# An attention step with cached keys and values on one core: two value tiles loaded as 120 and 8 rows, and the scores of the last three tiles ahead of their value products

## The chip, the cores and the metric

The kernel runs on one core of a Trainium2 chip. The metric is the time of one execution on the device in microseconds (us), as the median of several runs; less is better. Times in a profile count from the first instruction. The engines are named as in the profile: PE multiplies matrices, DVE and ACT work on vectors, POOL is nearly unused, and SP issues almost all transfers (DMA). Sixteen DMA engines carry the transfers.

## The reference

One decode step: four sequences, one query each, 32 heads, 4096 cached positions, head size 128, all in float32.

```python
x = A_x                                            # (4, 1, 512)
mod = (_silu(c) @ w_mod).reshape(c.shape[0], 6, 1, -1)
sa, ca, ga, sb, cb, gb = (mod[:, i] for i in range(6))
h = _layernorm(x) * (1 + ca) + sa
q = (h @ wq).reshape(4, 1, 32, 128)                # per head
scores = einsum("bhqd,bhkd->bhqk", q, k_cache) * 128 ** -0.5
o = einsum("bhqk,bhkd->bhqd", softmax(scores), v_cache)
x = x + ga * (o.reshape(4, 1, 4096) @ wo)
h = _layernorm(x) * (1 + cb) + sb
x = x + gb * (_silu(h @ w1) @ w2)                  # w1 (512, 1792), w2 (1792, 512)
```

The caches are 256 MB each. All that is read comes to 567 MB, and each byte is read once.

## The kernel before

**Tiles.** The work is cut into N = 64 steps. Step n = 4t + b takes two heads (2t and 2t + 1) of sequence b. Its keys are one tile of 128 partitions with 32 KB each (4 MB): 64 partitions for each head, and in a partition 64 positions of 128 values. Its values are a second tile of the same shape. I call them k*n* and v*n*.

**A step.** DVE multiplies the k tile by the query in two instructions (`mult`, L217). ACT sums 30 of the 64 positions (`red_act`, L223), DVE the other 34 (`red_dve`, L226), and that gives the scores. DVE takes the maximum of each partition (`rowmax`, L230), PE transposes the maxima (`bmax`, L234), DVE takes the maximum for each head and negates it (`negmax`, L241), ACT forms the exponentials (`softexp`, L252), and PE multiplies them with the v tile in 16 matmuls, each run as two passes (`pv`, L265, 32 in the profile). After four steps `finish_a` and `finish_b` divide by the sum and put the result of two heads into `oz`.

**The tail.** `project` multiplies `oz` with wo (L299), tile t by tile t; the first 12 of the 16 are done before the last `pv`. Then come the residual, the second layernorm, w1 (L357), SiLU, w2 (L367) and the output. The layernorm's result, transposed for the matmul with w1, is `h2T`.

**Buffers and order.** All big transfers go through one pool of five buffers of 32 KB per partition (`kv`), issued by SP in the order of the program (`fetch`, L71). A transfer into a buffer waits until the last reader of what was in it is done: a k buffer is freed by DVE and ACT, a v buffer by PE. The order on every engine is that of the program text; no scheduler moves instructions. Up to step 59 the tiles k(n+1) and v(n+1) are requested at the start of step n. For the last steps the order is k61, k62, k63 (at step 60), v61, v62 (at step 61), wo0 (step 62), the first half of wo1 (step 63, start), and, after the exponentials of step 63, v63 in three pieces, the rest of wo1 in two, w1, and w2 in four pieces. wo0 and wo1 are the halves of wo, 4 MB each; w1 and w2 have 3.5 MB each.

Of the kernel before, what the change touches and what calls it, by code (L numbers as in the profile page):

```python
# [17 lines left out]
def kernel(  # L18
# [14 lines left out]
    P = 128  # L33
    B, H, S, Dh = kc.shape
# [7 lines left out]
    NJ = HP * S // P  # L42
# [7 lines left out]
    EPS = 1e-5  # L50
    N = B * NT
    NP = 3

    const = ctx.enter_context(tc.tile_pool(name="const", bufs=1))
    kv = ctx.enter_context(tc.tile_pool(name="kv", bufs=5))
# [4 lines left out]
    def psum(shape, tag, bufs):  # L60
        return ps.tile(shape, F32, tag=tag, name=tag, bufs=bufs)
# [7 lines left out]
    def fetch(t, src, *cuts):  # L69
        for lo, hi in zip(cuts, cuts[1:]):  # L70
            nc.sync.dma_start(t[:, lo:hi], src[:, lo:hi])  # L71

    def load(name, shape, src, *cuts):
        t = kv.tile(shape, F32, tag="kv", name=name)
        fetch(t, src, *(cuts or (0, shape[1])))
        return t

    kt, vt = {}, {}

    def load_k(n):  # L80
        t, b = divmod(n, B)
        src = kc[b, HP * t : HP * (t + 1)].rearrange("h (p j) d -> (h p) j d", p=HALF)
        kt[n] = load(f"k{n}", [P, NJ, Dh], src)

    def load_v(n, *cuts):
        t, b = divmod(n, B)
        src = vc[b, HP * t : HP * (t + 1)].rearrange("h (p j) d -> (h p) j d", p=HALF)
        vt[n] = load(f"v{n}", [P, NJ, Dh], src, *cuts)

    xg = const.tile([P, P], F32, name="xg")  # L90
    cg = const.tile([P, P], F32, name="cg")
# [5 lines left out]
    for g in range(G):  # L97
        nc.gpsimd.dma_start(xg[W * g : W * g + B, :], xr[:, g * P : (g + 1) * P])
    wmt = [load(f"wm{i}", [P, 2, 6 * D], wmv[:, 2 * i : 2 * i + 2, :]) for i in range(2)]
    wqt = [load(f"wq{i}", [P, 2, H * Dh], wqv[:, 2 * i : 2 * i + 2, :]) for i in range(2)]  # L100
    load_k(0)
# [14 lines left out]
    for g in range(G):  # L116
        nc.vector.tensor_scalar(avg[:, g, :], sel, 1.0 / G, None, op0=ALU.mult)
    pz = [const.tile([P, NG * W + W // 2], F32, name=f"pz{i}") for i in range(NP)]
    for t in pz:
# [76 lines left out]
    def make_qb(t):  # L196
        p = psum([P, B, Dh], "q", 2)
        for b in range(B):
            for i in range(HP):
                ch, u = divmod(HP * t + i, CW // Dh)  # L200
                j, g = divmod(ch, G)
                nc.tensor.matmul(  # L202
                    p[HALF * i : HALF * (i + 1), b, :],
                    ident[:, W * g + b : W * g + b + 1].to_broadcast([P, HALF]),
                    qs[:, j, u * Dh : (u + 1) * Dh],
                    start=True, stop=True,
                )
        qb[t] = work.tile([P, B, Dh], F32, tag="qb", name=f"qb{t}")
        nc.scalar.activation(qb[t], p, AF.Copy)  # L209
# [3 lines left out]
    def mult(n, lo, hi):  # L213
        t, b = divmod(n, B)
        if lo == 0:
            sc[n] = work.tile([P, NJ], F32, tag="sc", name=f"sc{n}", bufs=3)
        nc.vector.tensor_mul(  # L217
            kt[n][:, lo:hi, :], kt[n][:, lo:hi, :], qb[t][:, b : b + 1, :].to_broadcast([P, hi - lo, Dh])
        )

    def red_act(n, lo, hi):
        for j in range(lo, hi):
            nc.scalar.activation(kt[n][:, j, :], kt[n][:, j, :], AF.Copy, accum_out=sc[n][:, j : j + 1])  # L223

    def red_dve(n, lo, hi):
        nc.vector.tensor_reduce(sc[n][:, lo:hi], kt[n][:, lo:hi, :], axis=AX.X, op=ALU.add)  # L226

    def rowmax(n):
        nm[n] = work.tile([P, 1], F32, tag="rm", name=f"rm{n}", bufs=3)
        nc.vector.tensor_reduce(nm[n], sc[n], axis=AX.X, op=ALU.max)  # L230

    def bmax(n):
        p = psum([P, P], "mx", 2)
        nc.tensor.transpose(p, nm[n].to_broadcast([P, P]), ident)  # L234
        nm[n] = p

    def negmax(n):
        t = work.tile([P, 1], F32, tag="nm", name=f"nm{n}", bufs=3)
        for i in range(HP):
            h = slice(HALF * i, HALF * (i + 1))  # L240
            nc.vector.tensor_reduce(t[h], nm[n][h, h], axis=AX.X, op=ALU.max, negate=True)  # L241
        nm[n] = t

    def softexp(n):
        t, b = divmod(n, B)
        if b == 0:
            rs[t] = work.tile([P, B], F32, tag="rs", name=f"rs{t}", bufs=3)
        o = W // 2 - JJ
        for i in range(HP):
            h = slice(HALF * i, HALF * (i + 1))  # L250
            w = pz[n % NP][h, : NG * W].rearrange("p (g w) -> p g w", w=W)
            nc.scalar.activation(  # L252
                w[:, :, o + i * W // 2 : o + i * W // 2 + JJ],
                sc[n][h].rearrange("p (g j) -> p g j", j=JJ),
                AF.Exp, bias=nm[n][h], accum_out=rs[t][h, b : b + 1],
            )

    def pv(n):
        t, b = divmod(n, B)
        if b == 0:  # L260
            po[t] = psum([P, JJ * Dh], "po", 2)
        o = W // 2 - JJ - JJ * b
        for j in range(NG):
            g = j % G
            nc.tensor.matmul(  # L265
                po[t][W * g : W * (g + 1), :],
                pz[n % NP][:, j * W + o : (j + 1) * W + o],
                vt[n][:, JJ * j : JJ * (j + 1), :].rearrange("p j d -> p (j d)"),
                start=(b == 0 and j < G), stop=(b == B - 1 and j >= NG - G),
            )  # L270

    def finish_a(t):
        o = work.tile([P, JJ, Dh], F32, tag="o", name="o")
        nc.vector.tensor_copy(o, po[t].rearrange("p (j d) -> p j d", j=JJ))  # L274
        d = psum([P, 1 + HP, B], "small", 1)
        nc.tensor.matmul(d[:, 0, :], blk, rs[t], start=True, stop=True)
        for i in range(HP):
            for r in range(HP):
                for j in range(JJ):
                    s = i * W // 2 + j  # L280
                    nc.tensor.matmul(  # L281
                        d[HALF * i : HALF * (i + 1), 1 + r, :], o[:, j, r::HP], sel[:, s : s + JJ * (B - 1) + 1 : JJ],
                        start=j == 0, stop=j == JJ - 1,
                    )
        sm[t] = d

    def finish_b(t):
        rd = work.tile([P, 1, B], F32, tag="rd", name="rd")
        nc.vector.reciprocal(rd, sm[t][:, 0:1, :])
        nc.vector.tensor_mul(oz[:, t, :, :B], sm[t][:, 1 : 1 + HP, :], rd.to_broadcast([P, HP, B]))  # L290
# [4 lines left out]
    def project(lo, hi):  # L295
        for t in range(lo, hi):
            for r in range(HP):
                for g in range(G):
                    nc.tensor.matmul(  # L299
                        accp[W * g : W * (g + 1), :], oz[:, t, r, :],  # L300
                        wot[t // NH][:, t % NH, r, g * P : (g + 1) * P],
                        start=(t == 0 and r == 0), stop=(t == NT - 1 and r == HP - 1),
                    )

    NH = NT // 2
    make_qb(0)
    load_v(0)
    for n in range(N):
        t, b = divmod(n, B)
        if n + 1 < N - 3:  # L310
            load_k(n + 1)
            load_v(n + 1)
        elif n == N - 4:
            load_k(N - 3)
            load_k(N - 2)
            load_k(N - 1)
        elif n == N - 3:
            load_v(N - 3)
            load_v(N - 2)
        elif n == N - 2:  # L320
            wot.append(load("wo0", [P, NH, HP, D], wov[:, :NH]))
        else:
            wot.append(load("wo1", [P, NH, HP, D], wov[:, NH:], 0, NH // 2))
        mult(n, 0, NA)
        if n >= B and b == 0:
            finish_a(t - 1)
        red_act(n, 0, NA)
        mult(n, NA, NJ)
        red_dve(n, NA, NJ)
        if n >= B and b == 0:  # L330
            finish_b(t - 1)
        rowmax(n)
        bmax(n)
        negmax(n)
        softexp(n)
        if n == N - 1:
            load_v(n, 0, NJ // 2, 3 * NJ // 4, NJ)
            fetch(wot[1], wov[:, NH:], NH // 2, 3 * NH // 4, NH)
            w1t = load("w1", [P, NK, F], w1v)
            w2t = load("w2", [P, NI, D], w2v, 0, 8, 12, 13, 14)  # L340
            project(0, NH + NH // 2)
        pv(n)
        if b == 1 and t + 1 < NT:
            make_qb(t + 1)
    finish_a(NT - 1)
# [56 lines left out]
```

## Time and profile before

| what | value |
|---|---|
| median of 3 runs | 1351.68 us (1351.64 to 1351.98) |
| the profiled execution | 1351.44 us |
| its span, first to last instruction | 1349.6 us |
| read from memory | 567.30 MB, 420 GB/s over the span |
| DVE, ACT, PE busy | 926.3, 643.8, 501.9 us |
| mean granted PE clock | 0.654 |

The busy rows of the page tell how long an engine worked in all; the slices tell when. The chain of work that ended last names, from the end backwards, what released each step. The stretches give for a time window each engine's busy time, the granted PE clock, the mean share of the sixteen DMA engines that was busy, and the rate.

### The profile page before, as it was taken

To read this page: it belongs to the slowest core of one execution; us is meant where nothing else is said; L and a number is where in the kernel's file an instruction comes from. 1 tells how busy PE (TensorE), PEld (TensorE's weight loads), DVE (VectorE), ACT (ScalarE), POOL (GpSimd) and SP (SyncE) were. 2 spreads that over 40 slices of the span, in tenths; PEclk is the share of its full clock that TensorE was granted. 3 is DMA by queue.
4 is the path that set the end of the run, shared out by engine and by line. 5 is a ranking of instruction groups with operands and counts; after the bars stand their busy time and mean duration, and the time that the engine had idled before them with its cause. 6 is when DMAs were issued, how large, how long until landed. Compare 5 with 4: busy or idle time off the path is not lost.

```text
span 1349.6 us, 12494 instructions
## 1 busy us (share of the span) xinstructions
PE 501.9 (37%) x3576; PEld 179.7 (13%) x3576; DVE 926.3 (69%) x468; ACT 643.8 (48%) x4129; POOL 5.5 (0%) x15
## 2 busy tenths in 40 slices
PE   4234323432432442343253333324323433433265
PEld 2011101110110111111011110101111110101033
DVE  1486677678668767766876776776686677668841
ACT  1354454455445445545544544554554455455530
POOL 1000000000000000000000000000000000000000
PEclk9666667657656666766666666666667556667567
DMA  9999999999999999999999999999999999999984
GB/s 404 433 431 427 431 434 430 427 431 434 429 428 432 433 429 427 433 432 431 430 431 433 428 429 432 433 430 428 431 433 429 431 431 429 430 433 431 418 336 177
DMA packets 22388, 568.10 MB, mean 421 GB/s; under 512 B 2432, under 2 KB 2480, under 8 KB 4784
## 3 DMA queue, kind: packets, MB, share of 16 engines
q1 hardware_dynamic: 22144, 567.29, 98.1%
q8 instruction: 28, 0.46, 0.1%
q14 instruction: 40, 0.33, 0.1%
q0 software_dynamic: 128, 0.01, 0.0%
q10 hardware_dynamic: 48, 0.01, 0.0%
HBM read 567.30 MB, written 0.01 MB: 420 GB/s over the span
## 4 chain that ended last, share of the span: by engine, by line
DMA 68%; DVE 17%; PE 12%; ACT 1%; SPq 1%; issue 1%; DVEq 0%; ACTq 0%
DMA k<-in_A_k_cache_dram 62%; DVE k L217 10%; PE po L265 10%; DVE sc L226 6%; DMA v<-in_A_v_cache_dram 3%; DMA w<-in_B_w_dram 2%; DMA wm<-in_w_mod_dram 1%; ACT pz L252 1%; SPq L71 1%; PE q L146 1%; PE mx L234 1%; PE q L357 0%; PE po L367 0%; DVE rm L230 0%; DVE nm L241 0%
## 5 line engine op out<-in xcount | busy, mean ns | idle before, releaser
L217 DVE TENSOR_TENSOR k<-k,qb 128x3840 f32<-128x3840 f32 (+1 forms) x128 | 561.9, 4421 | 309.0 <-DMA k<-in_A_k_cache_dram 308.9
L223 ACT ACTIVATE k<-k 128x128 f32<-128x128 f32 x1920 | 561.9, 294 | 396.4 <-DVE k L217 396.3
L265 PE MATMUL po<-v,pz 128*32 128x512 f32 x2048 | 367.4, 883 | 102.7 <-ACT pz L252 76.8
L223 ACT ACTIVATION_READ_ACCUMULATOR k<-k 128x1 f32 x1920 | 359.2, 187 | 0.0
L226 DVE TENSOR_REDUCE sc<-k 128x34 f32<-128x4352 f32 x64 | 299.9, 4686 | 2.2
L234 PE MATMUL mx<-ident,rm 128*128 128x128 f32 x64 | 28.5, 445 | 666.6 <-DVE rm L230 666.6
L265 PEld LDWEIGHTS po<-v,pz 128*32 128x32 f32 x2048 | 81.7, 154 | 346.2 <-issue 250.0
L234 PEld LDWEIGHTS mx<-ident,rm 128*128 128x128 f32 x64 | 11.6, 181 | 701.6 <-issue 674.0
L252 ACT ACTIVATE pz<-sc,nm 64x64 f32<-64x64 f32 x128 | 44.2, 345 | 126.2 <-DVE nm L241 124.6
L241 DVE TENSOR_REDUCE nm<-mx 64x1 f32<-64x64 f32 x128 | 28.4, 222 | 49.2 <-PE mx L234 47.3
L209 ACT ACTIVATE qb<-q 128x512 f32<-128x512 f32 x16 | 9.6, 597 | 102.6 <-PE q L202 102.6
L281 PE MATMUL small<-sel,o 128*64 128x4 f32 x512 | 42.0, 229 | 42.1 <-DVE o L274 42.1
L281 PEld LDWEIGHTS small<-sel,o 128*64 128x64 f32 x512 | 40.6, 186 | 43.5 <-DVE o L274 43.5
L252 ACT ACTIVATION_READ_ACCUMULATOR pz<-sc,nm 64x1 f32 x128 | 23.6, 185 | 0.0
L274 DVE COPY o<-po 128x512 f32<-128x512 f32 x16 | 11.1, 692 | 14.8 <-PE po L265 14.3
L230 DVE TENSOR_REDUCE rm<-sc 128x1 f32<-128x64 f32 x64 | 13.9, 217 | 5.4
L202 PE MATMUL q<-qs,ident 128*64 128x128 f32 x256 | 17.5, 279 | 0.0
L146 PE MATMUL q<-wm,csT 128*32 128x128 f32 x192 | 9.8, 386 | 17.1 <-DVE csT L131 13.5
L202 PEld LDWEIGHTS q<-qs,ident 128*64 128x64 f32 x256 | 13.6, 136 | 13.8 <-issue 13.8
L186 PE MATMUL q<-wq,hT 128*32 128x512 f32 x64 | 9.9, 773 | 6.8 <-DMA wq<-in_A_wq_dram 6.8
L299 PE MATMUL acc<-wo,oz 128*32 128x128 f32 x256 | 11.2, 346 | 0.1
L171 ACT ACTIVATE lnr<-mx,epst 128x1 f32<-128x1 f32 x2 | 0.5, 261 | 20.9 <-PE mx L169 20.9
(58 smaller groups left out, 81.1 us busy)
## 6 DMA issues: line engine op xcount, KB each, us to landing
k<-in_A_k_cache_dram SPq DMA_DIRECT2D x64, 4096.0 KB, 37.7
v<-in_A_v_cache_dram SPq DMA_DIRECT2D x63, 4096.0 KB, 35.7
wq<-in_A_wq_dram SPq DMA_DIRECT2D x2, 4096.0 KB, 36.7
wm<-in_w_mod_dram SPq DMA_DIRECT2D x2, 3072.0 KB, 10.1
wo<-in_A_wo_dram SPq DMA_DIRECT2D x1, 4096.0 KB, 36.5
w<-in_B_w_dram SPq DMA_DIRECT2D x1, 3584.0 KB
wo<-in_A_wo_dram SPq DMA_DIRECT2D x1, 2048.0 KB, 26.6
v<-in_A_v_cache_dram SPq DMA_DIRECT2D x1, 2048.0 KB
```

The costliest lines, as they stand in the source:

```text
L71: nc.sync.dma_start(t[:, lo:hi], src[:, lo:hi])
L146: nc.tensor.matmul(p[W * g : W * (g + 1), u, :], csT[:, k, :], wmt[k // 2][:, k % 2, o : o + P], start=k == 0, stop=k == NK - 1,)
L202: nc.tensor.matmul(p[HALF * i : HALF * (i + 1), b, :], ident[:, W * g + b : W * g + b + 1].to_broadcast([P, HALF]), qs[:, j, u * Dh : (u + ...
L217: nc.vector.tensor_mul(kt[n][:, lo:hi, :], kt[n][:, lo:hi, :], qb[t][:, b : b + 1, :].to_broadcast([P, hi - lo, Dh]))
L223: nc.scalar.activation(kt[n][:, j, :], kt[n][:, j, :], AF.Copy, accum_out=sc[n][:, j : j + 1])
L226: nc.vector.tensor_reduce(sc[n][:, lo:hi], kt[n][:, lo:hi, :], axis=AX.X, op=ALU.add)
L230: nc.vector.tensor_reduce(nm[n], sc[n], axis=AX.X, op=ALU.max)
L234: nc.tensor.transpose(p, nm[n].to_broadcast([P, P]), ident)
L241: nc.vector.tensor_reduce(t[h], nm[n][h, h], axis=AX.X, op=ALU.max, negate=True)
L252: nc.scalar.activation(w[:, :, o + i * W // 2 : o + i * W // 2 + JJ], sc[n][h].rearrange("p (g j) -> p g j", j=JJ), AF.Exp, bias=nm[n][h], ...
L265: nc.tensor.matmul(po[t][W * g : W * (g + 1), :], pz[n % NP][:, j * W + o : (j + 1) * W + o], vt[n][:, JJ * j : JJ * (j + 1), :].rearrange ...
L281: nc.tensor.matmul(d[HALF * i : HALF * (i + 1), 1 + r, :], o[:, j, r::HP], sel[:, s : s + JJ * (B - 1) + 1 : JJ], start=j == 0, stop=j == ...
```

## The change

First part: v21 and v42 (`SPLIT`, at one and two thirds of the 64 steps) are loaded in two transfers, partitions 0 to 119 and 120 to 127, into the same buffer. All other tiles are loaded as before. Second part: `pv(61)` and `pv(62)` move from the ends of steps 61 and 62 to step 63, behind its exponentials and its transfer requests and ahead of the first part of the projection.

```diff
+    FULL = 120
+    SPLIT = (N // 3, 2 * N // 3)
...
-    def load(name, shape, src, *cuts):
+    def load(name, shape, src, *cuts, rows=(0, P)):
         t = kv.tile(shape, F32, tag="kv", name=name)
-        fetch(t, src, *(cuts or (0, shape[1])))
+        for lo, hi in zip(rows, rows[1:]):
+            fetch(t[lo:hi], src[lo:hi], *(cuts or (0, shape[1])))
         return t
...
-        vt[n] = load(f"v{n}", [P, NJ, Dh], src, *cuts)
+        rows = (0, FULL, P) if n in SPLIT else (0, P)
+        vt[n] = load(f"v{n}", [P, NJ, Dh], src, *cuts, rows=rows)
...
         if n == N - 1:
             load_v(n, 0, NJ // 2, 3 * NJ // 4, NJ)
             fetch(wot[1], wov[:, NH:], NH // 2, 3 * NH // 4, NH)
             w1t = load("w1", [P, NK, F], w1v)
             w2t = load("w2", [P, NI, D], w2v, 0, 8, 12, 13, 14)
+        if n == N - 1:
+            pv(N - 3)
+            pv(N - 2)
             project(0, NH + NH // 2)
-        pv(n)
+        if n not in (N - 3, N - 2):
+            pv(n)
```

On SP, around v21 (here `v_1721`; the numbers are those of the buffers), before:

```order
L71 DMA v_1658<-in_A_v_cache_dram 128x8192 [waits DMAHW4_49,DVE_49,Activation_49]
L71 DMA k_1719<-in_A_k_cache_dram 128x8192 [waits DMAHW5_49,PE_49]
L71 DMA v_1721<-in_A_v_cache_dram 128x8192 [waits DMAHW6_49,DVE_49,Activation_49]
L71 DMA k_1807<-in_A_k_cache_dram 128x8192 [waits DMAHW7_49,PE_49]
L71 DMA v_1809<-in_A_v_cache_dram 128x8192 [waits DMAHW0_49,DVE_49,Activation_49]
```

and in the changed kernel:

```order
L73 DMA v_1658<-in_A_v_cache_dram 128x8192 [waits DMAHW4_49,DVE_49,Activation_49]
L73 DMA k_1719<-in_A_k_cache_dram 128x8192 [waits DMAHW5_49,PE_49]
L73 DMA v_1721<-in_A_v_cache_dram 120x8192 [waits DMAHW6_49,DVE_49,Activation_49]
L73 DMA v_1721<-in_A_v_cache_dram 8x8192
L73 DMA k_1808<-in_A_k_cache_dram 128x8192 [waits DMAHW7_49,PE_49]
```

The second transfer of 8 rows follows at once and waits for nothing more; what comes behind it has the same waits.

On PE, the last steps before (`v_4689` is v61, `v_4691` v62, `v_4858` v63, `wo_4752` and `wo_4813` the halves of wo):

```order
L234 MATMUL mx<-ident,rm_4727 128x128 [waits DVE_49,PE_49]
L265 MATMUL po<-v_4689,pz_112 32x512 [waits DMAHW5_49,Activation_49]
L265 MATMUL po<-v_4689,pz_112 32x512 x15
L234 MATMUL mx<-ident,rm_4788 128x128 [waits DVE_49,PE_49]
L265 MATMUL po<-v_4691,pz_113 32x512 [waits DMAHW6_49,Activation_49]
L265 MATMUL po<-v_4691,pz_113 32x512 x15
L234 MATMUL mx<-ident,rm_4849 128x128 [waits DVE_49,PE_49]
L299 MATMUL acc<-wo_4752,oz 32x128 [waits DMAHW7_49,Pool_49]
L299 MATMUL acc<-wo_4752,oz 32x128 x63
L299 MATMUL acc<-wo_4813,oz 32x128 [waits DMAHW0_49]
L299 MATMUL acc<-wo_4813,oz 32x128 x31
L265 MATMUL po<-v_4858,pz_111 32x512 [waits DMAHW1_49,Activation_49]
```

and in the changed kernel (the same tiles are `v_4691`, `v_4693`, `wo_4738` and `wo_4783`):

```order
L238 MATMUL mx<-ident,rm_4729 128x128 [waits DVE_49,PE_49]
L238 MATMUL mx<-ident,rm_4774 128x128 [waits DVE_49,PE_49]
L238 MATMUL mx<-ident,rm_4819 128x128 [waits DVE_49,PE_49]
L269 MATMUL po<-v_4691,pz_112 32x512 [waits DMAHW7_49,Activation_49]
L269 MATMUL po<-v_4691,pz_112 32x512 x15
L269 MATMUL po<-v_4693,pz_113 32x512 [waits DMAHW0_49,Activation_49]
L269 MATMUL po<-v_4693,pz_113 32x512 x15
L303 MATMUL acc<-wo_4738,oz 32x128 [waits DMAHW1_49,Pool_49]
L303 MATMUL acc<-wo_4738,oz 32x128 x63
```

The three transposed maxima now stand together, and both products behind the third.

On SP, the last transfers before:

```order
L71 DMA v_4691<-in_A_v_cache_dram 128x8192 [waits DMAHW1_49,PE_49]
L71 DMA wo_4752<-in_A_wo_dram 128x8x1024 [waits DMAHW2_49,DVE_49,Activation_49]
L71 DMA wo_4813<-in_A_wo_dram 128x4x1024 [waits DMAHW3_49,DVE_49,Activation_49]
L71 DMA v_4858<-in_A_v_cache_dram 128x4096 [waits DMAHW5_49,PE_49]
L71 DMA v_4858<-in_A_v_cache_dram 128x2048 x2
L71 DMA wo_4813<-in_A_wo_dram 128x2x1024 [waits DMAHW4_49]
L71 DMA wo_4813<-in_A_wo_dram 128x2x1024
L71 DMA w_4864<-in_B_w_dram 128x7168 [waits DMAHW6_49,PE_49]
L71 DMA w_4866<-in_B_w_dram 128x4096 [waits DMAHW7_49,DVE_49,Activation_49]
```

and in the changed kernel:

```order
L73 DMA v_4693<-in_A_v_cache_dram 128x8192 [waits DMAHW3_49,PE_49]
L73 DMA wo_4738<-in_A_wo_dram 128x8x1024 [waits DMAHW4_49,DVE_49,Activation_49]
L73 DMA wo_4783<-in_A_wo_dram 128x4x1024 [waits DMAHW5_49,DVE_49,Activation_49]
L73 DMA v_4828<-in_A_v_cache_dram 128x4096 [waits DMAHW6_49,DVE_49,Activation_49]
L73 DMA v_4828<-in_A_v_cache_dram 128x2048 x2
L73 DMA wo_4783<-in_A_wo_dram 128x2x1024
L73 DMA wo_4783<-in_A_wo_dram 128x2x1024 [waits DMAHW7_49]
L73 DMA w_4834<-in_B_w_dram 128x7168 [waits DMAHW0_49,PE_49]
L73 DMA w_4836<-in_B_w_dram 128x4096 [waits DMAHW1_49,PE_49]
```

v63 waited for PE (v61's buffer) and now waits for DVE and ACT (k63's buffer); w2 waited for DVE and ACT and now waits for PE. The DMAHW names are the semaphores of earlier transfers.

## The prediction

> **What bounds the kernel now.** I read the page first.
>
> ```profile
> span 1349.6 us, 12494 instructions
> PE 501.9 (37%) x3576; PEld 179.7 (13%) x3576; DVE 926.3 (69%) x468; ACT 643.8 (48%) x4129; POOL 5.5 (0%) x15
> ...
> GB/s 404 433 431 427 431 434 430 427 431 434 429 428 432 433 429 427 433 432 431 430 431 433 428 429 432 433 430 428 431 433 429 431 431 429 430 433 431 418 336 177
> ...
> q1 hardware_dynamic: 22144, 567.29, 98.1%
> q8 instruction: 28, 0.46, 0.1%
> q14 instruction: 40, 0.33, 0.1%
> ...
> DMA 68%; DVE 17%; PE 12%; ACT 1%; SPq 1%; issue 1%; DVEq 0%; ACTq 0%
> ...
> k<-in_A_k_cache_dram SPq DMA_DIRECT2D x64, 4096.0 KB, 37.7
> ...
> wo<-in_A_wo_dram SPq DMA_DIRECT2D x1, 4096.0 KB, 36.5
> ```
>
> No compute engine is busy for more than 69%, the DMA rate is flat near 430 GB/s for 37 slices, and DMA leads the chain: the kernel is bound by transfers. 430 GB/s over 16 engines is 26.9 GB/s each. A 4 MB tile has 128 rows of 32 KB, eight per engine, so a row takes 32768 B / 26.9 = 1.22 us and a tile 9.75 us. A k tile nevertheless lands 37.7 us after its issue: about four tiles stand in the queue.
>
> Second, SP's issues near the end (start, us until the last of them was issued).
>
> ```profile
> 1236.90 0.33 SPq L71 DMA_DIRECT2D k<-in_A_k_cache_dram  x1
> 1268.45 19.32 SPq L71 DMA_DIRECT2D wo<-in_A_wo_dram  x2
> 1291.14 7.20 SPq L71 DMA_DIRECT2D v<-in_A_v_cache_dram  x3
> 1298.38 5.19 SPq L71 DMA_DIRECT2D wo<-in_A_wo_dram  x2
> ```
>
> The last k tile is issued at 1236.90, wo0 at 1268.45 (with it the first half of wo1, later), v63's three pieces from 1291.14, the rest of wo1 from 1298.38.
>
> The third view, busy shares by stretch, shows the point of this case. Last two columns: DMA share of the 16 engines, GB/s.
>
> ```profile
> 100.00:400.00 300.00, 108.34 (x684) 35.91 (x688) 216.65 (x106) 149.47 (x971) 0.00 (x0) 0.64 1.00 430
> 1000.00:1270.00 270.00, 96.43 (x612) 32.72 (x612) 198.44 (x97) 137.75 (x897) 0.00 (x0) 0.63 1.00 430
> ...
> 1281.00:1282.00 1.00, 0.00 (x0) 0.00 (x0) 1.00 (x1) 1.00 (x9) 0.00 (x0) 0.50 0.93 373
> 1285.00:1286.00 1.00, 1.00 (x8) 0.37 (x12) 0.00 (x0) 0.00 (x0) 0.00 (x0) 0.50 0.57 233
> 1286.50:1288.40 1.90, 1.90 (x13) 0.48 (x9) 0.00 (x0) 0.00 (x0) 0.00 (x0) 0.50 0.08 34
> ...
> 1331.50:1341.80 10.30, 5.83 (x44) 2.10 (x48) 1.56 (x2) 0.54 (x1) 0.00 (x0) 0.67 0.06 25
> ```
>
> A share of 0.06 at 25 GB/s is one engine of sixteen. From 1331.5 to 1341.8 a single engine still works through its part of the last weights while fifteen are done. The same happens at 1286.5: fifteen engines have emptied everything issued so far, which is up to wo0. But wo0 as a whole lands 36.5 us after that, at 1304.95. So one engine is 1304.95 - 1286.5 = 18.5 us behind the last of the other fifteen, and a little more behind the first of them, which ran dry around 1282. A transfer counts as landed when its slowest part has landed, so this one engine paces every k tile of the body, and the other fifteen run ahead of it without ever standing idle (share 1.00).
>
> What delays it? Fetches of instructions are traffic that need not be spread over all sixteen. q14's 0.33 MB at 26.9 GB/s would take one engine 12 us, q8 and q14 together 29 us; the lag of 18.5 to 23 us lies between. That is an inference from sizes: no view tells which engine a fetch ran on.
>
> Fourth, the chain that ended last shows what the tail is paced by (start, us, what).
>
> ```profile
> 1249.04 35.81 DMA v<-in_A_v_cache_dram
> ...
> 1284.99 6.09 PE po L265 x32
> 1291.08 0.27 PE mx L234
> 1291.35 4.45 SPq L71
> ...
> 1303.67 29.87 DMA w<-in_B_w_dram
> 1333.54 0.14 issue
> 1333.68 5.25 PE q L357 x32
> ...
> 1341.19 4.95 PE po L367 x112
> ```
>
> v61 lands at V = 1284.85 (1249.04 + 35.81) and PE multiplies it; only then the transposed maximum of tile 62 (L234) can pass. w1 lands at 1333.54 = V + 48.7 and L357 follows; from there it is compute, 16.1 us to the end. I count the tail from V below.
>
> **The change, part by part.** *Two v tiles in 120 and 8 rows.* SP gains two issues. One costs 0.33 us, as for the k tile at 1236.90, and SP mostly waits for free tiles, so they are hidden; were SP the bound they would cost 0.66 us. Bytes are unchanged.
>
> What the split does to the engines no row shows, because no transfer of before has 120 rows, and no row numbers the engines. Bounds: 8 rows are one engine's share of a tile. If 120 rows go out as fifteen shares of eight, one engine gets nothing of them, and the other 8 rows go to eight engines, one each. (a) The engine left out is the slow one: it is spared 2 x 9.75 = 19.5 us, more than its lag. Then the last of the others paces, at 1286.5 instead of 1304.95 for wo0. Some of the others carry two rows more, 2 x 1.22 = 2.4 us; at 1285 to 1286 nine engines' worth is still running (0.57 x 16), so some of the loaded eight are nearly sure to be among the last. Gain 18.5 - 2.4 = 16.1 us at least, 18.5 at most. (b) The slow engine gets its eight rows as before and no extra: 0. (c) It is one of the eight with an extra row: 2.4 us lost. I take (a), at 16.1. The nearest row is that of the single engine at 0.06: the delayed engine is singular, and traffic that only one engine carries is most naturally put at an end of the row of sixteen, which is also where a left-out last share falls. That is a judgement, and its chance stands below.
>
> The Trainium skill's page "DMA: Bandwidth & Descriptors" (section on why a DMA increments its semaphore by 16) says that a transfer uses the largest number of engines up to 16 that divides its rows, the lowest-numbered ones: 15 for 120 rows, 8 for 8 rows. By that the last engine is left out, case (a) if it is the slow one. Its section "Latency and other measured facts" says that engines 7 and 15 are usually slower; here one engine lags, not two, and which it is no run here shows. By engine 15 the sum is (a), by engine 7 it is (c).
>
> *The products of v61 and v62 wait for the scores of v63's tile.* The rows of DVE and PE:
>
> ```profile
> 1283.44 0.22 DVE L230 TENSOR_REDUCE rm<-sc 128x1 f32<-128x64 f32 x1
> 1291.37 0.47 DVE L241 TENSOR_REDUCE nm<-mx 64x1 f32<-64x64 f32 x2 [7.71 <-PE mx L234]
> 1291.88 8.76 DVE L217 TENSOR_TENSOR k<-k,qb 128x3840 f32<-128x3840 f32 x2
> 1305.47 0.22 DVE L230 TENSOR_REDUCE rm<-sc 128x1 f32<-128x64 f32 x1
> ...
> 1294.78 6.32 PE L265 MATMUL po<-v,pz 128*32 128x512 f32 x32 [3.44 <-DMA v<-in_A_v_cache_dram]
> 1305.84 0.45 PE L234 MATMUL mx<-ident,rm 128*128 128x128 f32 x1 [4.75 <-DVE rm L230]
> 1306.21 8.01 PE L299 MATMUL acc<-wo,oz 128*32 128x128 f32 x192
> 1315.05 1.92 PE L265 MATMUL po<-v,pz 128*32 128x512 f32 x16 [0.83 <-DMA v<-in_A_v_cache_dram]
> 1317.44 1.07 PE L265 MATMUL po<-v,pz 128*32 128x512 f32 x8 [0.47 <-DMA v<-in_A_v_cache_dram]
> 1319.95 1.07 PE L265 MATMUL po<-v,pz 128*32 128x512 f32 x8 [1.44 <-DMA v<-in_A_v_cache_dram]
> ...
> 1330.57 0.40 DVE L131 STREAM_TRANSPOSE h2T<-hg 128x128 f32<-128x128 f32 x1
> ```
>
> Removed: DVE's 7.71 us wait behind v61's product. Tile 63's multiply would start about 7 us earlier, at V, and its row maximum (13.6 us later, as 1305.47 - 1291.88) at V + 13.6; the transposed maximum is over at V + 14.4. Added: PE does v61's product only then (6.1 us), then v62's (6.3), until V + 26.8, then 8.0 us of projection, until V + 34.8. Before, projection ended at V + 29.4, so PE is 5.4 us later there. v63's last quarter is multiplied from 1319.95 = V + 35.1 to V + 36.2; now the 4.1 us of that product (1.92 + 1.07 + 1.07) follow the projection and end at V + 38.9, 2.7 us later. Everything up to h2T follows: before it was ready at 1330.97 and L357 waited 2.6 us more for w1. So 2.7 - 2.6 = 0.1 us reaches the end. At half the granted clock throughout (0.50 in the stretches above; these three pieces already ran mostly there) perhaps 3 more; if PE runs at full clock, nothing.
>
> Transfers moved by it: v63 now takes k63's place instead of v61's and is issued after L226 of tile 63, at V + 13.5 instead of V + 6.3 (1291.14). The transfer engines come to it after wo0 (1304.95 = V + 20.1) and 2 MB of wo1 (4.9 us): V + 25. So 11 us of cover; without it each us would show. SP needs 12.4 us (7.2 + 5.2) for v63 and the rest of wo1, until V + 25.9, past v61's product at V + 20.5, so w1 is issued near V + 26 and w2 near V + 28 (before: 1303.67 = V + 18.8). Engines reach w1 14.6 us after V + 25 (6 MB), at V + 39.6: 13 us of cover. w2's last piece lands near V + 57, as before (the single engine's work ends at 1341.8), while L367 begins at 1341.19 = V + 56.3 and takes the pieces in their order. Here fifteen engines no longer run ahead and starve, so their idle stretch around 1287 goes too; it lay off the pacing engine and is worth nothing by itself.
>
> **Sum.** Gain 16.1 from the split, loss 0.1 for PE's order, nothing for the issues: 16.0 us. The profiled execution took 1351.44 us (1.84 beside its span of 1349.6), 0.24 below the median of 1351.68. 1351.44 - 16.0 = 1335.4, or 1335.7 as a median.
>
> **The rivals.**
> *PE becomes the end of the tail* (faster, less). For it: after the change the products of v61 and v62, the projection and v63's product stand in one row on PE, and slack is down to nothing. Price 3 to 8 us of the 16, if the granted clock stays at 0.50: 1339 to 1344. It decides from 2.6 us of delay on. Against: they ran at that clock before.
>
> *The engine left out is not the slow one*, (b) or (c): 1351.7 or 1354.1, with the 0.1 above. For it: nothing numbers the engines. The Trainium skill's same page ("Rules for kernel authors") says not to bother with two transfers to disjoint parts of the partitions, since both use the same engines; by that rule it is case (b). It speaks of halves, which divide evenly; no run here shows it.
>
> *Slower: 120 rows go out as eight shares of 15.* Eight engines then carry 16 rows of each split tile instead of 8, 2 x 9.75 = 19.5 us more, on one engine in two. If the slow one is among them it decides at once: 1351.7 + 19.5 = 1371; if not, those eight take its place, 19.5 against a lead of 18.5, which is about 1352.7. It decides when the loaded engine has less than 19.5 us of lead. Against: fifteen shares need no more than even division.
>
> **How the numbers follow.** Within 0.2% (2.7 us) a measurement of this kernel can hardly tell from no change. (a) as summed: 0.71, own range 1332 to 1340 (all 18.5 us, and w1 0.6 us earlier by its bytes, at V + 48.1: 1332.6; PE 4 us late: 1340). PE as the end: 0.09, 1339 to 1344, with the open 2 us of the gain to 1346. Another engine left out: 0.13, of it 0.11 within 0.2% (0 to 2.5 us lost), 0.02 slower, where extra rows and a later PE add up to more than 2.7 us. Eight shares: 0.07, all slower or near it. So faster 0.80, same 0.11, slower 0.09. The range 1332 to 1346 holds the first two, 0.80.
>
> **What would show it.** Right: in the stretches near the end no long one at 0.06; k's issue-to-landing is shorter than before in relation to what is queued, and its last landings are about 16 us earlier; w1 lands near 1317.5 and L357 starts within a us of it; DVE's 7.71 us wait for L234 of tile 62 is gone. Wrong: 0.06 still stands for 10 us or more (another engine was left out), or a share near 0.5 stands there (eight loaded engines), or L357 waits for h2T by several us (PE's order costs).

## The result, and the profile after

The changed kernel takes 1405.87 us (median of 4 runs, 1403.25 to 1409.46) against 1351.66 us before: a ratio of 1.0403, interval 1.0378 to 1.0429. It is 54 us slower, where 16 us less were forecast. The profiled execution took 1403.25 us with a span of 1401.4, 51.8 more than before.

The page of the changed kernel, the lines that answer to those shown of before (busy time, 40 slices, queues, shares of the chain):

```profile
span 1401.4 us, 12497 instructions
PE 495.5 (35%) x3576; PEld 175.9 (13%) x3576; DVE 926.2 (66%) x468; ACT 643.9 (46%) x4129; POOL 5.5 (0%) x15
...
DMA  9999999999999999999999999998999999999965
GB/s 404 434 432 427 425 434 433 433 430 428 429 433 431 230 425 429 433 429 428 430 432 429 432 430 430 234 382 368 411 421 429 419 419 427 425 426 426 409 269 220
...
q1 hardware_dynamic: 22158, 567.29, 97.5%
...
q14 instruction: 40, 0.33, 0.1%
...
DMA 63%; DVE 20%; PE 11%; another core or an unknown queue 3%; ACT 1%; issue 1%; SPq 0%; DVEq 0%; ACTq 0%
```

The busy times are nearly those of before (PE 495.5 us instead of 501.9), and the bytes are the same. What changed is the rate: 230 in slice 14 and 234 in slice 26, and then 382 and 368, where before all stood near 430. The DMA row beside it still says 9: the engines were busy, they only moved half as much. A slice is 1401.4 / 40 = 35.0 us, so slice 14 lost 35 x (430 - 230) / 430 = 16.3 us, slice 26 16.0, slices 27 to 37 together 14: 46 of the 52 us lie in these slices.

SP's issues of the two split tiles (v21, v42), two pieces in each row:

```profile
436.62 0.75 SPq L73 DMA_DIRECT2D v<-in_A_v_cache_dram  x2
...
874.73 0.69 SPq L73 DMA_DIRECT2D v<-in_A_v_cache_dram  x2
```

The stretches behind them (PE, PEld, DVE, ACT, POOL, granted clock, DMA share, GB/s):

```profile
455.00:460.00 5.00, 0.80 (x5) 0.38 (x9) 3.16 (x6) 2.07 (x13) 0.00 (x0) 0.50 1.09 242
460.00:465.00 5.00, 5.00 (x28) 1.11 (x24) 0.00 (x0) 0.00 (x0) 0.00 (x0) 0.54 1.02 216
475.00:480.00 5.00, 0.00 (x0) 0.00 (x0) 5.00 (x2) 4.26 (x29) 0.00 (x0) 0.50 0.92 138
480.00:485.00 5.00, 0.00 (x0) 0.00 (x0) 4.94 (x2) 4.61 (x32) 0.00 (x0) 0.50 0.93 223
...
895.00:900.00 5.00, 0.00 (x0) 0.00 (x0) 0.00 (x0) 0.54 (x4) 0.00 (x0) 0.50 1.16 210
900.00:905.00 5.00, 3.69 (x20) 1.13 (x24) 0.00 (x0) 0.00 (x0) 0.00 (x0) 0.51 0.80 151
...
1385.00:1390.00 5.00, 4.85 (x29) 1.49 (x32) 0.00 (x0) 0.00 (x0) 0.00 (x0) 0.54 0.07 30
```

About 20 us after a split tile is issued, which is when the engines come to it, they run at about half rate with a share near 1 (0.80 to 1.16). At half rate 4 MB take 20 us, but the rate is low for 30, with the least at 475 (138); the section on `halves_early` says why. The last row shows that the lone engine (share 0.07) is still there at the end.

The trace also keeps when each engine's share of a transfer has landed, which no view lists. The 120 rows of v21 land as fifteen shares, about 20 us after those of k21, the tile ahead: eight rows each, 2.5 us a row. Fourteen are there between 474.9 and 482.5 us, the fifteenth at 492.6. The 8 rows land as eight shares, seven between 477.5 and 485.2 us and one at 494.9. So the slow engine has a part of both.

The chain around the first split and at the end:

```profile
425.20 46.27 DMA k<-in_A_k_cache_dram
...
1356.77 28.25 DMA w<-in_B_w_dram
1385.02 0.14 issue
1385.15 5.44 PE q L365 x32
```

The k tile issued at 425.20, ahead of v21, needs 46.3 us instead of some 38. w1 lands at 1385.02 instead of 1333.54, 51.5 us later: the loss is complete before the tail begins, and the tail itself costs what it did. The 3% of "another core or an unknown queue" are waits that this view ties to no transfer; one of them, 17.93 us from 486.41, ends when k22 is there.

### The profile page after: what moved, and what is told of

Same layout as the page of the kernel before. It is cut to its first block, busy times and chain, and to the rows that moved or that the text cites. A ratio compares the mean times of both kernels' runs of the same rounds, so it can differ in the third digit from the quotient of the medians.

```text
span 1401.4 us, 12497 instructions
## 1 busy us (share of the span) xinstructions
PE 495.5 (35%) x3576; PEld 175.9 (13%) x3576; DVE 926.2 (66%) x468; ACT 643.9 (46%) x4129; POOL 5.5 (0%) x15
## 4 chain that ended last, share of the span: by engine, by line
DMA 63%; DVE 20%; PE 11%; another core or an unknown queue 3%; ACT 1%; issue 1%; SPq 0%; DVEq 0%; ACTq 0%
DMA k<-in_A_k_cache_dram 58%; DVE k L221 13%; PE po L269 9%; DVE sc L230 7%; DMA wq<-in_A_wq_dram 3%; DMA w<-in_B_w_dram 2%; ACT pz L256 1%; PE mx L238 1%; PE q L190 0%; PE q L365 0%; PE po L375 0%; DVE nm L245 0%; DVE rm L234 0%; DVE o L278 0%
## 5 line engine op out<-in xcount | busy, mean ns | idle before, releaser
L234 DVE TENSOR_REDUCE rm<-sc 128x1 f32<-128x64 f32 x64 | 13.9, 217 | 5.4
```

## The experiments

### The two parts, each alone

`split_only` has the two split tiles and the old order of PE, `order_only` the new order and no split.

```diff
 split_only:  +        rows = (0, FULL, P) if n in SPLIT else (0, P)   # FULL = 120
 order_only:  +            pv(N - 3); pv(N - 2)      (step 63, ahead of project)
              -        pv(n)
              +        if n not in (N - 3, N - 2): pv(n)
```

> The kernel before with v21 and v42 loaded as 120 and 8 rows, nothing else. If the split alone costs the 54 us: 1402 to 1410 us. If the later products at the end cost a part of it: clearly less, 1352 to 1395.

> The kernel before with the products of v61 and v62 behind the scores of step 63, and no split. My prediction priced this at 0.1 us: 1350 to 1354 us. If the order is harmful: 1360 or more.

Split alone: 1403.19 us against 1351.75, ratio 1.0391 (1.0374 to 1.0408). Order alone: 1351.45 us, ratio 0.9996 (0.9986 to 1.0005). So the whole loss is the split's, and the order is neutral. The order's rows in `order_only`, DVE and PE:

```profile
1284.49 0.47 DVE L245 TENSOR_REDUCE nm<-mx 64x1 f32<-64x64 f32 x2 [0.63 <-PE mx L238]
...
1330.59 0.40 DVE L135 STREAM_TRANSPOSE h2T<-hg 128x128 f32<-128x128 f32 x1
...
1299.33 9.17 PE L269 MATMUL po<-v,pz 128*32 128x512 f32 x64
1308.32 5.41 PE L303 MATMUL acc<-wo,oz 128*32 128x128 f32 x192
1315.14 1.92 PE L269 MATMUL po<-v,pz 128*32 128x512 f32 x16 [1.40 <-DMA v<-in_A_v_cache_dram]
```

DVE's wait of 7.71 us for L234 of tile 62 is down to 0.63. The two products take 9.17 us where 6.1 + 6.3 were priced, the projection 5.41 where 8.0 was; PE is done before v63 lands (it waits 1.40 us for it), and h2T is there at 1330.99, 0.02 us later than before. The chain of `order_only` shows w1's landing:

```profile
1305.13 28.44 DMA w<-in_B_w_dram
1333.57 0.14 issue
```

### Halves: is it the number fifteen, or the set of partitions?

`halves` cuts the same two tiles at 64, so that each piece has 64 rows, which divide evenly over sixteen.

```diff
-    FULL = 120
+    FULL = 64
```

> The kernel before with v21 and v42 loaded as 64 and 64 rows instead of 120 and 8. Theory P (what costs is which partitions are written at the same time: a block of 64 adjacent partitions is only half of the memory's entrances): both halves run near half the rate, about 215 GB/s, some 10 us more for each of the two tiles, 1365 to 1380 us. Theory F (what costs is a number of rows that sixteen does not divide, so that fifteen and eight engines work): 64 rows go over sixteen engines, full rate, 1350 to 1354 us.

1397.2 us, ratio 1.0336 (1.032 to 1.0351). Even division doesn't help: a piece on half of the partitions is slow too. The stretch after the first split in `halves`:

```profile
456.00:476.00 20.00, 5.50 (x33) 1.33 (x33) 5.52 (x7) 1.20 (x7) 0.00 (x0) 0.67 1.02 205
```

All sixteen are busy (1.02) and move 205 GB/s, 0.48 of 430. That is what the partition theory says. The size was missed: 45.5 us for two tiles, 22.7 each, where 4 MB at 205 instead of 430 GB/s cost 20.5 - 9.75 = 10.7. The Trainium skill's page "SBUF — State Buffer" (section on Door 1, the DMA port swizzle) states that partitions 0 to 63 reach only eight of sixteen ports and 64 to 127 the other eight, so that 64 partitions get about half the rate of 128; it gives 196 GB/s as measured at 1 MB and about 218 as the limit. The 205 measured here agrees.

### Heads: two transfers, all partitions in each

`heads` loads the same two tiles in two transfers of 2 MB as well, but each over all 128 partitions.

```diff
+            for i in range(HP):
+                one = vc[b, HP * t + i].rearrange("(p j) d -> p j d", p=P)
+                nc.sync.dma_start(vt[n][:, NJ // 2 * i : NJ // 2 * (i + 1)], one)
```

> The kernel before with v21 and v42 loaded in two transfers of 2 MB, the same two halves of the source as in the run with 64 and 64 rows (one head each), but each spread over all 128 partitions, 16 KB per partition. (The rows of these two tiles then meet other weights than they should; that part of the result is another.) If what costs is the partitions that are written at the same time: full rate, 1350 to 1354 us. If it is the reading of one 2 MB region by all engines: as with 64 and 64 rows, 1390 to 1400 us.

1352.05 us, ratio 1.0007 (0.9998 to 1.0017): no loss. The stretch where the engines come to it:

```profile
460.00:480.00 20.00, 7.91 (x41) 1.75 (x44) 14.11 (x6) 9.75 (x64) 0.00 (x0) 0.59 1.02 436
```

436 GB/s, where the changed kernel moved 190 in the same 20 us. Two transfers cost nothing and neither does cutting a tile; between `halves` and `heads`, what costs is which partitions are written at the same time. For the changed kernel itself this is not shown as far: its 120 rows are fifteen sixteenths of the partitions and still ran at half rate, no view tells which of them were written together, and no run loads the 120 or the 8 rows alone.

### Halves early: why a tile costs twice what its rate says

The lag of 18.5 us was read at the end of the run. By the shares in the trace of before it grows along the way: the last share of a tile lands 0.1 us after the last but one at k3, 4.3 us at k21, 10.3 at k42 and 17.9 at v61. `halves_early` cuts v2 and v3 at 64, where the engines are still in step.

```diff
-    SPLIT = (N // 3, 2 * N // 3)
+    SPLIT = (2, 3)
```

> 64 and 64 rows as before, but for v2 and v3 instead of v21 and v42, when the slow engine is only about 2 us behind. If a split tile costs twice, once when the others are in it and once when the slow engine is (20 us apart late in the run): about half of the 45 us, 1368 to 1380 us, since here both fall together. If it costs a fixed amount per tile: 1392 to 1400 us.

1375.52 us, ratio 1.018 (1.0165 to 1.0195): 24.3 us or 12.1 a tile, against 22.7 for v21 and v42 in `halves`; the rate alone gives 10.7. What the rest is, the changed kernel shows. DVE starts a multiplication when its k tile is there; these are k21 and k22, then k42 and k43, before:

```profile
462.79 8.76 DVE L217 TENSOR_TENSOR k<-k,qb 128x3840 f32<-128x3840 f32 x2 [3.71 <-DMA k<-in_A_k_cache_dram]
482.93 8.76 DVE L217 TENSOR_TENSOR k<-k,qb 128x3840 f32<-128x3840 f32 x2 [5.22 <-DMA k<-in_A_k_cache_dram]
...
878.64 8.76 DVE L217 TENSOR_TENSOR k<-k,qb 128x3840 f32<-128x3840 f32 x2 [5.21 <-DMA k<-in_A_k_cache_dram]
898.99 8.76 DVE L217 TENSOR_TENSOR k<-k,qb 128x3840 f32<-128x3840 f32 x2 [5.43 <-DMA k<-in_A_k_cache_dram]
```

and in the changed kernel:

```profile
471.50 8.76 DVE L221 TENSOR_TENSOR k<-k,qb 128x3840 f32<-128x3840 f32 x2 [12.64 <-DMA k<-in_A_k_cache_dram]
504.36 8.76 DVE L221 TENSOR_TENSOR k<-k,qb 128x3840 f32<-128x3840 f32 x2 [17.95 <-DMA k<-in_A_k_cache_dram]
...
917.59 8.76 DVE L221 TENSOR_TENSOR k<-k,qb 128x3840 f32<-128x3840 f32 x2 [22.76 <-DMA k<-in_A_k_cache_dram]
949.51 8.76 DVE L221 TENSOR_TENSOR k<-k,qb 128x3840 f32<-128x3840 f32 x2 [17.00 <-DMA k<-in_A_k_cache_dram]
```

k21 isn't split and was issued ahead of v21, yet it comes 8.7 us late: fifteen engines are in v21 by then, and the slow one, still in k21, is held up with them. When the slow engine is through its own rows of v21, k22 is 21.4 us late. At the second split k42 is 39.0 us late and k43 50.5. So a split tile is paid once while the others are in it and once more when the slow engine comes to its own rows, and it is dearer the further behind that engine is: 21.4 us for v21 with 4.2 us of lag and 29.1 for v42 with 12.2, the lags again by the shares. Why the slow engine is held up in a whole tile is not shown.

### Probes: which engine lags?

`probe` adds small loads of 1 to 15 rows, which nothing reads, behind v(n+1) in steps 30 to 59. It takes 1350.16 us in one run, so no cost of theirs shows. `probe_read` lets POOL copy a column of each (1 to 8 rows, steps 44 to 59).

```diff
+                m = (n - 44) % 8
+                nc.sync.dma_start(probe[m][: m + 1], wqv[: m + 1, 0, :P])
+                nc.gpsimd.tensor_copy(seen[m][: m + 1], probe[m][: m + 1, 0:1])
```

> The kernel before with one small transfer behind each v request of steps 30 to 59: 1 to 15 rows of 512 bytes (tiles ta to to: 1 row to 15 rows) into tiles that nothing reads. A transfer of r rows that goes to the first r engines lands when the slowest of these r gets to it. If the slow engine is the last of sixteen, all probes of 2 to 15 rows land 13 to 25 us after issue, before the v tile ahead of them (about 36 us). If it is the one at place i (from 1), probes with fewer than i rows land early and those with i rows or more at about 36 us. Time of the kernel: 1350 to 1356 us in all cases.

> The probes of the run before, 1 to 8 rows, behind the v requests of steps 44 to 59, and POOL (otherwise idle there) copies one column of each as soon as it has landed, so that its landing shows as the end of a POOL wait. If the second engine is the slow one: the 1-row probe is read about 22 us after its issue, each probe of 2 to 8 rows about 36 us after it. If a later one of the first eight: 3 and more rows late too only from that one on. If none of the first eight: all near 20 us. Time of the kernel: 1349 to 1354 us.

1352.57 us, one run. SP's issues and POOL's copies in `probe_read`; ta has one row, tb two, th eight:

```profile
1071.30 0.28 SPq L317 DMA_DIRECT2D ta<-in_A_wq_dram  x1
1091.56 0.28 SPq L317 DMA_DIRECT2D tb<-in_A_wq_dram  x1
1209.62 0.33 SPq L317 DMA_DIRECT2D th<-in_A_wq_dram  x1
...
1088.45 0.17 POOL L318 COPY ua<-ta 1x1 f32<-1x1 f32 x1 [1.44 <-DMA ta<-in_A_wq_dram]
1127.23 0.18 POOL L318 COPY ub<-tb 2x1 f32<-2x1 f32 x1 [38.60 <-DMA tb<-in_A_wq_dram]
1245.98 0.18 POOL L318 COPY uh<-th 8x1 f32<-8x1 f32 x1 [19.88 <-DMA th<-in_A_wq_dram]
```

One row is there 17.2 us after its issue, two rows after 35.7, eight after 36.4. So a transfer of one row misses the slow engine and one of two rows meets it. The shares in the trace of `probe` say so for up to fifteen rows: one row lands after 19 to 25 us, and of each load of 2 to 15 rows exactly one share comes late, after 34.8 to 36.3 us. That the landings of one row and of two rows lie 18.5 us apart, the very lag read at the end of the run, is chance: of the fifteen rows issued at 1210.05, the slow share lands 17.3 us after the last of the others and 22.0 after the first.

By the Trainium skill's page "DMA: Bandwidth & Descriptors" (section on why a DMA increments its semaphore by 16) a transfer takes the lowest-numbered engines; with these rows that makes the slow one the second of sixteen. Then the fifteen of the 120 rows include it, and so do the eight of the 8 rows: the prediction's case (c), and the shares of v21 agree. The Trainium skill's note on the same page that engines 7 and 15 are usually the slow ones, which it puts down, as a guess, to transfers issued by GpSimd, doesn't hold here, where SP issues them.

### Does instruction fetch delay that engine?

q14 fetches instructions in 40 packets, and ACT's row of the page has the most instructions (4129 of 12494). `act8` lets ACT sum 8 instead of 30 positions in steps 0 to 59, DVE the other 56; `act8_filled` then gives ACT the lost 22 pairs of instructions back on a constant tile, and `act8_again` gives them back on the k tile itself.

```diff
 act8:         +        na = 8 if n < N - 4 else NA      # NA = 30
 act8_filled:  +        for _ in range(NA - na):
               +            nc.scalar.activation(junk, ident, AF.Copy, accum_out=junks)
 act8_again:   +            same = kt[n][:, i % na, :]    # i from 0 to NA - na
               +            nc.scalar.activation(same, same, AF.Copy, accum_out=junks)
```

> The kernel before, with ACT summing 8 instead of 30 of the 64 positions in steps 0 to 59, and DVE the other 56: some 2600 of ACT's 4129 instructions go, DVE's sum gets about 3 us longer a step (17.9 of the 19.7 us period). If the slow engine is late because it also fetches ACT's instructions: q14 falls from 40 packets to about 20, the lag from 18.5 to 8 to 10 us, and the time to 1340 to 1345 us. If the lag has another cause: 1350 to 1355 us.

> act8, and ACT runs in each of the steps 0 to 59 the 22 instruction pairs that it lost, of the same form, on a constant tile that nothing else uses. DVE and the transfers have the same work as in act8. If act8 is faster because less is fetched for ACT: q14 is back at 40 packets, the single engine is late again and the time back at 1349 to 1354 us. If act8 is faster for another reason (less work on ACT's critical steps, or another timing of the buffers): 1337 to 1341 us.

> As the kernel with 8 positions on ACT in steps 0 to 59, but ACT runs the 22 pairs per step that fell away once more over the first 8 positions of the k tile, in place (a copy of the same values, the sum goes to a spare column). So ACT has its old number of instructions, and its old traffic on the buffers of the transfers, whereas in the run with a constant tile that traffic was gone, and there the rate stood at 431 to 433 GB/s instead of 430 to 431. Theory that the fetch delays one engine, and that the constant tile's run was 0.5% (about 6 us) faster for want of ACT's traffic on the k tile: lag as before, rate 430 to 431, 40 packets on q14, 1346 to 1352 us. Theory that DVE's cut of 8 and 56 positions gives the gain, whatever ACT does: 1338 to 1342 us with the rate at 432 or more.

`act8`: 1338.01 us, ratio 0.9904 (0.9889 to 0.9919). `act8_filled`: 1341.13, ratio 0.9933 (0.9917 to 0.9949). `act8_again`: 1342.85, ratio 0.9933 (0.9916 to 0.9949). The page of `act8`, its queue of fetches and the chain's shares:

```profile
q14 instruction: 20, 0.16, 0.0%
...
DVE 55%; DMA 27%; PE 14%; issue 2%; ACT 1%; SPq 1%; DVEq 0%; ACTq 0%
```

Its stretches in the body and at the end:

```profile
100.00:400.00 300.00, 104.51 (x679) 32.87 (x679) 263.21 (x103) 51.69 (x303) 0.00 (x0) 0.64 1.00 430
1326.00:1329.00 3.00, 1.16 (x25) 1.15 (x29) 1.56 (x2) 0.16 (x1) 0.00 (x0) 0.84 0.07 25
1329.00:1334.00 5.00, 3.77 (x94) 3.50 (x84) 0.58 (x2) 0.00 (x0) 0.00 (x0) 0.76 0.00 0
```

The page of `act8_filled`, and then its stretches, at the end and in the body:

```profile
q14 instruction: 40, 0.33, 0.1%
...
DMA 44%; DVE 38%; PE 15%; issue 1%; ACT 1%; SPq 0%; DVEq 0%
```

```profile
1324.00:1334.00 10.00, 6.13 (x90) 2.88 (x93) 2.05 (x4) 1.35 (x2) 0.00 (x0) 0.78 0.07 27
100.00:400.00 300.00, 107.60 (x679) 33.59 (x679) 261.88 (x103) 186.93 (x987) 0.00 (x0) 0.61 1.00 433
```

The stretches of `act8_again` (its q14 has 40 packets too):

```profile
1323.00:1334.00 11.00, 6.84 (x59) 2.93 (x63) 3.05 (x8) 2.09 (x3) 0.00 (x0) 0.66 0.06 25
100.00:400.00 300.00, 109.93 (x679) 33.48 (x679) 261.25 (x103) 187.20 (x988) 0.00 (x0) 0.61 1.00 432
```

Two things must be held apart. The lag follows the fetch: with 20 packets the lone engine works for 3 us at the end (share 0.07), with 40 packets for 10 to 11, as before, whatever ACT reads. By the shares, the last of v61 lands 17.9 us after the last but one in before, 3.2 in `act8`, 14.8 in `act8_filled` and 15.1 in `act8_again`. The trace of before shows it packet by packet. Of the 126 intervals between the last shares of two k or v tiles, the median is 9.72 us and 31 are longer than 10 (10.4 us on average). A packet of q14 starts in each of these 31, and in 5 of the other 95. So most packets set the slow engine back by 0.7 us; a packet itself takes 0.31, and what the rest is stays open. In `act8` only 8 intervals are that long: most of the 20 packets that are left don't hold the slow engine up, and the lag fell below the expected 8 to 10 us. It is worth its length: v61's last share lands 14.2 us earlier than before, the last but one 0.7 us later, and the time falls by 13.3, to below the 1340 to 1345 us expected.

The time doesn't follow the fetch in the same way: 1349 to 1354 us, and 1346 to 1352 for `act8_again`, were expected from the fetch theory, and both stayed 9 to 10 us under the time before (the other theories' 1337 to 1341 and 1338 to 1342 were missed by less than 1 us). In the body these two run at 432 to 433 GB/s where before and `act8` show 430; 0.5% of 1300 us is 6.5 us, most of that gain. ACT's traffic on the k tile isn't the reason, since `act8_again` has it back. DVE's cut of 8 and 56 positions alone isn't either, since `act8` has it and stays at 430. What raises the rate stays open.

### Toward a faster kernel

`act8_order` is `act8` with the new order of PE, `act4_order` the same with 4 positions on ACT.

```diff
 act8_order:  +        na = 8 if n < N - 4 else NA       and order_only's lines
 act4_order:  +        na = 4 if n < N - 4 else NA       and order_only's lines
```

> act8 with the second part of the change, the products of v61 and v62 behind the scores of step 63. By the run with the order alone (ratio 0.9996): the same as act8 within 2 us, 1336 to 1340 us. If the order gains now that the slow engine no longer sets the tail: 1330 to 1335 us.

> act8_order with 4 instead of 8 positions on ACT in steps 0 to 59. If the lag still paces the end: 1 to 2 us faster than act8_order. If DVE, with some 18.5 us of work in a step of 19.5, takes over as the bound: the same or up to 5 us slower.

`act8_order`: 1337.32 us, ratio 0.9901 (0.9887 to 0.9916), the fastest here, 14 us below before and 69 below the changed kernel; from `act8` alone it can't be told apart. `act4_order`: 1357.41 us, ratio 1.0045 (1.0032 to 1.0058), 20 us above `act8_order` where 5 at most were expected. Its page:

```profile
PE 484.4 (36%) x3576; PEld 165.3 (12%) x3576; DVE 1134.3 (84%) x468; ACT 188.2 (14%) x1009; POOL 5.5 (0%) x15
...
DVE 78%; PE 12%; DMA 7%; issue 2%; ACT 1%; DVEq 0%; SPq 0%; ACTq 0%
```

DMA's share of the chain falls from 68% to 7% and DVE's rises from 17% to 78%: with 60 of the 64 positions on DVE it sets the pace of the step, and the transfers wait for buffers.

## Why the prediction was wrong

**The step that failed** is the split's term, 16.1 us of gain, which measured 51.4 us of loss (`split_only`). Two things in it were wrong.

- The choice of (a). The engine left out of the 120 rows isn't the slow one; the probes put the slow one in any transfer of two rows or more, and one share of the 120 rows of v21 lands 10 us after the other fourteen. Case (c) was on the list, at 2.4 us, and would have given 1354.1.
- What none of the three cases held: the rate. "Bytes are unchanged" was taken to mean that a row still costs 1.22 us. The term counted rows per engine and never asked where those rows are written. In the pieces the engines ran with a share near 1 at 138 to 242 GB/s, and a row of v21 took 2.5 us. `halves` shows the same with even division, and `heads` shows full rate with two transfers over all partitions. Nor did the term hold that the slow engine, still in the tile ahead, is held up as well. This step is worth about 50 us and decides the sign. Why 120 rows, nearly all partitions, run as slowly as 64 stays open.

The prediction weighed the Trainium skill's rule (page "DMA: Bandwidth & Descriptors", section "Rules for kernel authors") that two transfers to disjoint partitions aren't worth the trouble, and took it as case (b), no change. That rule names no price. For `halves` the price is in the Trainium skill's rule on ports cited there; for 120 rows that rule by itself does not give one.

**The lag** was read rightly: one engine of sixteen, 18.1 us behind the last of the others in wo0 by the shares (wo0 lands 36.5 us after its issue at 1268.45, not after 1286.5, as the sentence there reads; the difference taken from it is right). That instruction fetch is its cause was an inference from sizes, 12 us for q14 and 29 with q8; the 31 long intervals and the run with 20 packets bear it out for q14, at 0.7 us a packet. That a shorter lag is worth its length, as case (a) supposed, `act8` shows: 14.2 us less on the last share, 13.3 us less time.

**The order on PE** was priced at a loss of 0.1 us; 0.3 us of gain, inside the interval, was measured. Its parts were too dear (12.4 us of products took 9.17, 8.0 of projection 5.41; the granted clock was 0.77 from 1299 to 1309 and 1.00 from 1308 to 1314, near the full clock for which the prediction had seen no delay), so the predicted 2.7 us delay of h2T was 0.02. The covers held: w1 landed at 1333.57 in `order_only`, 0.03 us from before.

**The rivals.** "Slower" had the sign but another mechanism (eight shares of fifteen rows); its 1371 would have asked for idle engines beside eight busy ones, and the share stood near 1. PE didn't become the end. Of the signs of being wrong, "0.06 still stands" came true: from 1386 the lone engine works alone for some 8 us. The signs of being right failed: w1 was to land near 1317.5 and landed at 1385.02.

## What to carry to other kernels

Keep every big transfer on all 128 partitions. When a transfer must be cut, cut along the row, as `heads` does, at no cost; a cut by partitions ran at half rate and cost 12 us for a 4 MB tile, about twice that where the engines were out of step. A DMA share of 1.0 doesn't mean full rate: read the GB/s beside it. And when an engine falls behind the others, count the instructions before touching the transfers: taking 2640 of ACT's 4129 away halved the fetches, cut the lag from 18 to 3 us and brought 13 us, where DVE had room for the work.

## What the hardware showed that was not expected

- Sixteen busy engines that write only half of the partitions move 205 GB/s instead of 430; with 120 and 8 rows it is 138 to 242.
- The price of such a tile depends on how far the engines are out of step: 12.1 us a tile for 64 and 64 rows when they are together; for 120 and 8 rows 21.4 us with a lag of 4.2 and 29.1 with 12.2.
- One engine, met by transfers of two rows and missed by those of one, is late by 18 us near the end of the run. The lone stretch at the end shrinks from some 10 us to 3 when q14 has 20 packets instead of 40; most packets cost that engine 0.7 us, though they take 0.31.
- With the sums divided anew and ACT's number of instructions kept, the body's rate was 432 to 433 GB/s; with the same division and fewer instructions, and before, it was 430. No run explains this.
